# Sixteen stores moved from ScalarE's queue to GpSimd's, and four small moves of work in an attention and experts kernel

## The chip, the cores and the metric

The kernel runs on one core of a Trainium2 chip. The metric is the device time of one execution in microseconds (us), the median of several runs. The engines are TensorE (PE in the profile; PEld is its weight load), VectorE (DVE), ScalarE (ACT), GpSimd (POOL) and SyncE (SP), which issues DMAs. PEq, ACTq and SPq are the engines' sequencers.

## What is computed

The reference chains three blocks (float32; batch B = 2, 768 rows of each, 8 heads of 64, so rows of 512):

```python
# 1. attention: a window of n_local keys behind each row, and n_global keys for all
scores = scale * q @ k.T + bias; scores = where(keep, scores, -1e9)
a = exp(scores - max); a /= sum(a) + 1e-9;  x = a @ v
# 2. one expert of 8 for each row; a row whose local gate is >= 0.5
#    keeps the expert of the row before it
e = argmax(x @ w_gate) if s == 0 or local_gate < 0.5 else prev_e
p = softmax(x @ w_gate);  out[s] = p[e] * (relu(x[s] @ w1[e]) @ w2[e])
# 3. theta, mixing over the 768 rows, output
theta = x @ w_theta; y = w_tok_r @ (x * cos(theta)) + w_tok_i @ (x * sin(theta))
u = x + y; return u + relu(u @ w_ch)
```

## The kernel before

**Attention, 0 to about 99 us.** 24 steps s, each with two units u = 2s and 2s + 1. PE multiplies queries by keys (`s`, L554); DVE adds the bias and takes the maximum in one operation (`sm` with its read-out `st`, L576); ACT exponentiates (`pr`, L586); PE transposes (`pt`, L609); ACT or DVE copies the result (`ps`, L616 and L618); PE multiplies by the values (`x`, L633). Work of a finished block of 128 rows is put at places of later steps by `at(...)`: in an odd step DVE scales the block (`xt`, L659) and later makes the gate logits (`lh`, L231). Each engine takes its instructions in the order in which the code issues them. Two pieces of PSUM are shared in turn by PE's transposes and the small products of the gate, so the second group of `pt` in an odd step can only begin when DVE has read what `lh` reads.

**Jobs.** The weights of block 3 arrive as 64-bit numbers and are turned to float32 bit by bit in "jobs", sequences of one ACT operation (`jm`, L401) and DVE operations (`jw`, L402 to L408; `wtok` L411 and L414). `job_tick()` issues one piece. In attention it is called at the end of the steps in `JATT` (L71).

**Warm products.** Before the first query product PE runs `NWARM` products of a zero tile (`warm`, L858) whose result nobody reads.

**Experts, about 118 to 298 us.** Rows are sorted by expert, gathered from `xd` into tiles (`xg`, L1026, an indirect DMA on POOL), transposed, and run through 8 experts r of 8 parts f each, so u = 8r + f counts 64 parts. The weights `raw` come from SP's queue; ACT and DVE split each into two halves (`w1s` L1346 and L1347, `w2s` L1444 and L1445) for PE (`h` L1463 and L1480, `o` L1536). From r = 4 two parts are run together. `probs()` (L1049 to L1056, seven DVE operations and one of ACT) works out each row's probability once, after part `PU`, and SP stores the table to DRAM (`pd`, L1693). POOL gathers it for each group of rows (`ps`, L1388; for expert 0 from part `GP`). `y_rows` scales an expert's result by it on ACT (`yo`, L1586, two buffers) and stores it to `yd` (L1588). The first 128 rows ("leader's rows") are worked out ahead of the experts in `y0`; `gather_p0` fetches their probabilities after part `HU`, and `y_head` scales and stores them at `HU + 4` (L1591, L1592). At the end POOL gathers rows from `yd` (`rows`, L1408) for `first` (L1428).

**Theta, mix and output, 298 to 476 us**, close to all of it on PE.

Of the kernel before, what the change touches and what calls it, by code (L numbers as in the profile page):

```python
# [50 lines left out]

BLOCKS = [b * NT + t for t in range(NT) for b in range(B)]
TWO_PI = 6.283185307179586
NWARM = 10

WARM = {0: 1, 1: 2, 2: 1, 3: 1, 4: 1}

# [13 lines left out]
JATT = (4, 5, 6, 8, 9, 10, 12, 13, 14, 16, 17, 18, 20, 21, 22)  # L71
# [7 lines left out]
FT = 4  # L79
JF, JL = 4, 56  # L80
LOADS = ((0, 2), (1, 1), (2, 1), (1, 2), (2, 2))
PU = 1
GX = 0
XF = 3
GP = 4
HU = 36
XL = 0
S1A, S1B = 0, 0
C1 = 6.28125
# [11 lines left out]
def kernel(  # L101
# [13 lines left out]
    V, A, G, PE, SP = nc.vector, nc.scalar, nc.gpsimd, nc.tensor, nc.sync  # L115
# [6 lines left out]
    def ct(shape, dt, name):  # L122
        return const.tile(shape, dt, name=name, tag=name)
# [3 lines left out]
    yd = dram.tile([NSLOT * 128, DM], F32, name="yd", tag="yd")  # L127
# [265 lines left out]
    def job(k):  # L393

        t = jraw.pop(k)
        lo, hi = t[:, :, 0], t[:, :, 1]
        w = jtmp.tile([128, 512], I32, tag="jw", name="jw", bufs=1)
        m = jtmp.tile([128, 512], F32, tag="jm", name="jm", bufs=1)
        wf = w.bitcast(F32)
        wh, wl = jobs[k][1]()  # L400
        A.activation(m, hi.bitcast(F32), AF.Abs)  # L401
        V.tensor_scalar(w, hi, 3, 0x3FFFFFFF, op0=ALU.logical_shift_left, op1=ALU.bitwise_and)  # L402
        yield
        V.scalar_tensor_tensor(w, lo, 29, w, op0=ALU.logical_shift_right, op1=ALU.bitwise_or)  # L404
        yield
        V.scalar_tensor_tensor(w, hi, -1073741824, w, op0=ALU.bitwise_and, op1=ALU.bitwise_or)
        yield
        V.scalar_tensor_tensor(wf, m, MIN64, wf, op0=ALU.is_ge, op1=ALU.mult)  # L408
        yield
        wf = wf.rearrange("p (i c) -> p i c", c=wh.shape[-1]) if len(wh.shape) == 3 else wf  # L410
        A.activation(wh, wf, AF.Copy)  # L411
        job_load()
        yield
        jstate["sub"].tensor_tensor(wl, wf, f32(wh), op=ALU.subtract)  # L414

    def job_tick(n=1):
        for _ in range(n):
            if jstate["gen"] is None:
                if jstate["k"] not in jraw:
                    return  # L420
                jstate["gen"] = job(jstate["k"])
                jstate["k"] += 1
            if next(jstate["gen"], 0) == 0:
                jstate["gen"] = None
# [10 lines left out]
    y0 = ct([128, DM], F32, "y0")  # L435
# [6 lines left out]
    with ExitStack() as actx:  # L442
# [11 lines left out]
        def load_qk(i):  # L454
            n = BLOCKS[i]
            b, t = divmod(n, NT)
            q = qs[n] = ab.tile([128, 4, 128], F32, tag="q", name="q", bufs=3)
            src = pack[b, t, :, 0:1152].rearrange("p (j c) -> p j c", j=4)
            o = 0 if t else 32

            for j in (slice(0, 2), slice(2, 4)) if n == 0 else (slice(0, 4),):
                SP.dma_start(q[:, j], src[:, j, 0:128])
                SP.dma_start(kall[:, b, j, t * 160 + o : t * 160 + 160], src[:, j, 128 + o : 288])

        def load_v(i):
            n = BLOCKS[i]
            vv = ab.tile([128, 2, 512], F32, tag="vv", name="vv", bufs=4)
            src = pack[n // NT, n % NT]
            if n % NT:
                SP.dma_start(vv, src[:, 1152:2176].rearrange("p (i c) -> p i c", i=2))  # L470
            else:
                SP.dma_start(vv[:, 1], src[:, 1664:2176])
            vals[n] = vv
# [44 lines left out]
        def biases(t, j):  # L518
            bias, c = (bias1, slice(128, 384)) if t else (bias0, slice(0, 128))
            for h in (2 * j, 2 * j + 1):  # L520
                (G if t else V).tensor_scalar(bias[:, h], drop[:, c], -8.0 * 2.0 ** -(h + 1), None, op0=ALU.mult)
# [22 lines left out]
        def qk(s):  # L544
            n = units[2 * s][0]
            b, t = divmod(n, NT)
            W = 256 if t else 128
            for i in range(2):

                sp = [pS.tile([128, 256], F32, tag=f"s{hh}", name=f"s{hh}") for hh in range(2)]  # L550
                j = units[2 * s + i][1]
                for hh in range(2):
                    half = slice(64 * hh, 64 * hh + 64)
                    PE.matmul(  # L554
                        sp[hh][:, 0:W],
                        lhsT=qs[n][half, j],
                        rhs=kall[half, b, j, t * 160 + 160 - W : t * 160 + 160],
                        start=True,
                        stop=True,
                    )  # L560
                ust[2 * s + i] = {"s": [x[:, 0:W] for x in sp]}
# [291 lines left out]
        def warm(k):  # L853

            if k:
                w = pM.tile([128, 512], F32, tag="m", name="warm")
            for _ in range(k):
                PE.matmul(w, lhsT=wm[:, 0:128], rhs=wm, start=True, stop=True)  # L858
# [53 lines left out]
        def run(names):  # L912
            for k in names.split():
                ops[k]()
# [5 lines left out]

        warm(NWARM)
        biases(0, 0)
# [5 lines left out]
        for s in range(NS):  # L928
            if s % 2 == 0 and s // 2 + 2 < NB and s:
                load_qk(s // 2 + 2)  # L930
                load_v(s // 2 + 2)
            u = 2 * s
            qk(s)
            warm(WARM.get(s, 0))
            run(later.pop((s, 0), ""))
            run(f"sa{u} sb{u}")
            run(later.pop((s, 1), ""))
            if s:
                run(f"tr{u - 2} tr{u - 1} cp{u - 2}")
            run(f"sa{u + 1} sb{u + 1}")  # L940
            if s:
                run(f"cp{u - 1}")
            run(later.pop((s, 2), ""))
            if s == 0:
                biases(0, 2)
                biases(0, 3)
            if s >= 2:
                run(f"pv{u - 4} pv{u - 3}")
                if s % 2:
                    i, t = s // 2 - 1, (s // 2 - 1) // B  # L950
                    at(s + 1, 0, f"ev{i}")
                    at(s + 1, 2, f"ri{i}")
                    at(s + 1, 3, f"yt{i} lg{i}")
                    at(s + 2, 0, f"lc{i} lt{i} ys{i}")
                    at(s + 2, 1, f"ld{i}")
                    if i % B == B - 1:
                        at(s + 2, 2, f"ch{t}")
                        at(s + 3, 0, f"ro{t}")
                        at(s + 3, 1, f"sc{t}")
                        at(s + 4, 0, f"oh{t}")  # L960
                        at(s + 4, 1, f"ho{t}")
                        at(s + 5, 0, f"po{t}")
                        at(s + 5, 1, f"pl{t}")
                        at(s + 5, 2, f"mk{t}")
                        at(s + 6, 3, f"sl{t}")
                        at(s + 7, 1, f"tk{t}")
                        if B * (t + 1) == AHEAD:
                            at(s + 5, 2, "le " + " ".join(f"lw{f}" for f in range(8)))
                            at(s + 7, 1, "lx ls")
            run(later.pop((s, 3), ""))  # L970
            if s in (1, 2):
                job_load()
            if s in JATT:
                job_tick()
            if s in FILLS:
                fill()
# [387 lines left out]
    with ExitStack() as mctx:  # L1364
# [209 lines left out]
        def groups_out(n, M, W):  # L1574

            return yd[n : n + M, :].rearrange("m (g c) -> g m c", c=W)

        def y_rows(r, lo, hi):
            for i in range(lo, hi):
                c = width(r, i)  # L1580
                M = min(128, RCAP[r] - i * 128) if c == 128 else c
                P, W = (M, DM) if c == 128 else (128, 4 * c)
                ps = pslot.pop(RBASE[r] + i)[:P]
                yo = mb.tile([128, DM], F32, tag="yo", name="yo", bufs=2)
                yp = yps[r][i]
                A.activation(yo[:P, :W], yp[:P, :W], AF.Copy, scale=ps)  # L1586
                n = (RBASE[r] + i) * 128
                A.dma_start(groups_out(n, M, W), yo[:P, :W])  # L1588

        def y_head():  # L1590
            A.activation(y0, y0, AF.Copy, scale=pslot.pop(0))  # L1591
            A.dma_start(yd[0:128, :], y0)  # L1592

        def y_last():
            yo = first["yo"] = pre.tile([128, DM], F32, tag="w1s0", name="yo", bufs=3)
# [23 lines left out]
        for u in range(64):  # L1619
# [68 lines left out]
            if GX <= u < GX + RTILES[0]:  # L1688
                gather_x(RBASE[0] + u - GX + 3)
            if u == PU:  # L1690
                probs()
                for b in range(B):
                    SP.dma_start(pd.rearrange("(t b p) o -> b p (t o)", b=B, p=128)[b], ptok[:, b * NT : (b + 1) * NT])  # L1693
            if f == 0:
                slots_of_groups(r)
            i = f - (1 if r else GP)
            if 0 <= i < RTILES[r]:
                gather_p(r, i)
            if u == HU:
                gather_p0()  # L1700
            if u == HU + 4:
                y_head()
# [384 lines left out]
```

## Time and profile before

| | us |
|---|---|
| median of 3 runs (lowest, highest) | 480.87 (480.5, 482.27) |
| profiled execution, whole | 482.78 |
| its span, from first to last instruction | 481.0 |
| attention / rest of its tail / experts / block 3 | 99 / 19 / 180 / 178, then 5 us of stores |

The span is what the profiler's rows cover; 1.8 us lie around it. A row of a timeline has the start, the busy time, the engine, the line, the operation, the tile written and those read, the form, how often it ran in a row, and in brackets how long the engine was idle before it and what released it.

### The profile page before, as it was taken

The page shows a single profiled execution, that of the slowest core. Times are in us where ns is not written, and L with a number is a line of the kernel's source. Part 1 is how long each engine was busy: PE and PEld are TensorE (multiplying, and loading weights), DVE is VectorE, ACT ScalarE, POOL GpSimd, SP SyncE. Part 2 cuts the span into 40 slices and gives each one's busy share as a digit, 9 for nine tenths or more (in the row PEclk, how much of TensorE's full clock was granted, in tenths as well). Part 3 has the DMA queues.
Part 4 walks back from the last instruction along what each step waited for, and adds up shares of the span by engine and source line. Part 5 has one row for each costly group of instructions (what it writes and reads, how often), then busy time and mean ns, then how long its engine had stood idle before and what let it go on. Part 6 is the DMA issues. An engine that isn't in the chain of part 4 may idle for free.

```text
span 481.0 us, 9458 instructions
## 1 busy us (share of the span) xinstructions
PE 467.0 (97%) x3311; PEld 382.3 (79%) x3311; DVE 348.5 (72%) x913; ACT 256.5 (53%) x615; POOL 125.5 (26%) x173
## 2 busy tenths in 40 slices
PE   8999998999999999999999999999999999999995
PEld 4676776778878798888876778788888888888885
DVE  5878878867667788877685876566999899761521
ACT  5978786732445757665555464554655455520300
POOL 8502213224105303020312011203444233340400
PEclk9999999999999999999999999999999999999999
DMA  8978677524939978887998994610012200000022
GB/s 232 369 218 266 180 243 245 196 89 122 348 56 278 312 267 262 291 259 251 292 296 272 314 302 155 188 38 22 23 67 67 65 23 22 1 33 35 33 79 90
DMA packets 62370, 82.96 MB, mean 172 GB/s; under 512 B 6528, under 2 KB 40960, under 8 KB 62320
## 3 DMA queue, kind: packets, MB, share of 16 engines
q1 hardware_dynamic: 54068, 62.66, 40.7%
q10 hardware_dynamic: 5500, 12.85, 7.9%
q0 software_dynamic: 2752, 6.83, 4.9%
q8 instruction: 27, 0.44, 0.4%
q14 instruction: 23, 0.19, 0.1%
HBM read 70.94 MB, written 11.38 MB: 171 GB/s over the span
## 4 chain that ended last, share of the span: by engine, by line
PE 76%; DVE 8%; DMA 7%; ACT 4%; issue 2%; ACTq 1%; SPq 0%; DVEq 0%; POOLq 0%
PE a L1846 21%; PE o L1536 9%; PE h L1480 7%; PE b L1883 7%; PE th L1770 6%; PE h L1463 4%; DMA raw<-in_w_dram 4%; PE x L633 3%; PE s L554 3%; PE pt L609 3%; DMA yd<-yo 3%; DVE sm L576 2%; ACT pr L586 2%; PE y L775 2%; PE h L764 2%
## 5 line engine op out<-in xcount | busy, mean ns | idle before, releaser
L1846 PE MATMUL a<-wtokr,z 128*128 128x512 f32 x480 | 85.9, 337 | 0.0
L1846 PEld LDWEIGHTS a<-wtokr,z 128*128 128x128 f32 x480 | 73.8, 188 | 9.3
L1536 PE MATMUL o<-w2s,hh 128*128 128x512 f32 x192 | 63.6, 409 | 0.8 <-DVE w2s L1445 0.4
L586 ACT ACTIVATE pr<-sm,st 128x256 f32<-128x256 f32 (+1 forms) x96 | 46.0, 481 | 16.7 <-DVE st L576 15.5
L1480 PE MATMUL h<-xT,w1s 128*128 128x288 f32 (+3 forms) x384 | 52.6, 285 | 2.0 <-DVE w1s L1347 1.1
L1480 PEld LDWEIGHTS h<-xT,w1s 128*128 128x128 f32 x384 | 48.8, 189 | 5.8 <-DVE w1s L1347 2.0
L1445 DVE TENSOR_TENSOR w2s<-raw,w2s 128x512 fp32r<-128x512 f32 x56 | 38.5, 687 | 18.9 <-ACT w2s L1444 11.4
L576 DVE CUSTOM_DVE_ANT_0 sm<-s,bias 128x256 f32<-128x256 f32 (+1 forms) x96 | 33.9, 394 | 11.7 <-PE s L554 10.2
L1026 POOL DMA_INDIRECT xg<-xd,xidx x17 | 17.2, 1013 | 95.3 <-PE tr L1318 88.6
L1463 PEld LDWEIGHTS h<-xT,raw 128*128 128x128 f32 x256 | 37.0, 190 | 4.4 <-issue 3.9
L1463 PE MATMUL h<-xT,raw 128*128 128x192 f32 (+3 forms) x256 | 40.5, 311 | 0.0
L1536 PEld LDWEIGHTS o<-w2s,hh 128*128 128x128 f32 x192 | 32.3, 184 | 8.3 <-DVE w2s L1445 2.7
L1536 PE MATMUL o<-w2s,hl 128*128 128x512 f32 x96 | 38.0, 396 | 0.8 <-DVE hl L1511 0.8
L1444 ACT ACTIVATE w2s<-raw 128x512 fp32r<-128x512 f32 x56 | 34.9, 625 | 6.0 <-PE o L1536 3.6
L1347 DVE TENSOR_TENSOR w1s<-raw,w1s 128x512 fp32r<-128x512 f32 x32 | 22.0, 690 | 9.7 <-ACT w1s L1346 9.4
L1891 DVE SCALAR_TENSOR_TENSOR ob<-b,xTf 128x512 f32<-128x512 f32 (+1 forms) x16 | 8.8, 556 | 27.2 <-PE b L1883 27.1
L609 PE MATMUL pt<-ident,pr 128*128 128x128 f32 x176 | 26.1, 281 | 1.8 <-DVE lh L231 0.7
L1802 POOL TENSOR_TENSOR si<-si,yg 128x512 f32<-128x512 f32 x10 | 13.5, 1346 | 51.6 <-ACT si L1795 48.7
L411 ACT ACTIVATE wtokr<-jw 128x512 fp32r<-128x512 f32 x15 | 9.5, 631 | 31.4 <-DVE jw L408 29.5
L554 PE MATMUL s<-kall,q 64*128 64x256 f32 (+1 forms) x192 | 26.0, 388 | 0.1
L404 DVE SCALAR_TENSOR_TENSOR jw<-jraw,jw 128x512 int32<-128x512 int32 x26 | 24.7, 952 | 0.4
L633 PE MATMUL x<-ps,vv 128*64 128x128 f32 x352 | 24.5, 279 | 0.0
(286 smaller groups left out, 952.3 us busy)
## 6 DMA issues: line engine op xcount, KB each, us to landing
raw<-in_w_dram SPq DMA_DIRECT2D x60, 512.0 KB
vv<-in_pack_dram SPq DMA_DIRECT2D x10, 512.0 KB
jraw<-in_w_tokT_dram ACTq DMA_DIRECT2D x10, 512.0 KB
w<-in_w_dram SPq DMA_DIRECT2D x16, 256.0 KB
kall<-in_pack_dram SPq DMA_DIRECT2D x10, 320.0 KB
xd<-xt SPq DMA_DIRECT2D x12, 256.0 KB
q<-in_pack_dram SPq DMA_DIRECT2D x11, 256.0 KB
jraw<-in_w_tokT_dram ACTq DMA_DIRECT2D x10, 256.0 KB
```

The costliest lines, as they stand in the source:

```text
L554: PE.matmul(sp[hh][:, 0:W], lhsT=qs[n][half, j], rhs=kall[half, b, j, t * 160 + 160 - W : t * 160 + 160], start=True, stop=True,)
L576: V.tensor_tensor_reduce(out=sm[:, hh, 0:W], in0=ust[u]["s"][hh], in1=bias[:, 2 * j + hh], scale=-0.125, scalar=BIG, op0=ALU.add, op1=ALU.min,
L586: A.activation(pr[:, hh, 0:W], sm[:, hh, 0:W], AF.Exp, bias=st[:, hh : hh + 1], scale=-1.0, accum_out=sums[n][:, 2 * j + hh : 2 * j + hh + 1],
L609: PE.transpose(pt[:, hh, c], pr[:, hh, c * 128 : (c + 1) * 128], ident)
L633: PE.matmul(xp[64 * hh : 64 * hh + 64, j], lhsT=vv[:, i, h * 64 : (h + 1) * 64], rhs=ps[:, hh, c], start=(c == 0), stop=(c == nch - 1),)
L1444: A.activation(h2, bb[:, o], AF.Copy)
L1445: V.tensor_tensor(l2, bb[:, o], f32(h2), op=ALU.subtract)
L1463: PE.matmul(hp[:, :N], lhsT=pieces[u // 2][1][:, j, o * 128 : (o + 1) * 128], rhs=x[:, j, :N], start=(j == 0), stop=(j == 3),)
L1480: PE.matmul(hp[:, :N], lhsT=wa[:, j], rhs=xa[:, j, :N], start=(k == 0), stop=(k == 11))
L1536: PE.matmul(out[:M], lhsT=ha[:, lo : lo + M], rhs=wa, start=(f == 0 and q == 0), stop=(f == 7 and q == 2),)
L1846: PE.matmul(acc[b][d][o], lhsT=za[:, d * 128 : (d + 1) * 128], rhs=wa[:, lo:hi], start=(t == 0 and n == 0 and (o == 0 or d % 2 == 0)), sto ...
L1883: PE.matmul(op[:, : hi - lo], lhsT=wa[:, d, e * 128 : (e + 1) * 128], rhs=ua[d][:, lo:hi], start=(n == 0), stop=(n == 11),)
```

## The change

Five edits. `NWARM` goes from 10 to 7. `probs()` and the store of its table come after part 3 rather than part 1, and POOL's gathers of expert 0's probabilities start one part later. `gather_p0` comes after part 32 and `y_head` after part 36 rather than 36 and 40. All 16 stores of results to `yd` in `y_rows` and `y_head` are issued by POOL (`G`) rather than ACT (`A`). And the `job_tick()` of an even attention step is issued in the odd step after it, behind that step's first `sm` operations.

```diff
-NWARM = 10
+NWARM = 7
-PU = 1
+PU = 3
-GP = 4
-HU = 36
+GP = 5
+HU = 32
             run(f"sa{u} sb{u}")
+            if s % 2 and s - 1 in JATT:
+                job_tick()
             run(later.pop((s, 1), ""))
...
-            if s in JATT:
+            if s % 2 and s in JATT:
                 job_tick()
...
                 n = (RBASE[r] + i) * 128
-                A.dma_start(groups_out(n, M, W), yo[:P, :W])
+                G.dma_start(groups_out(n, M, W), yo[:P, :W])

         def y_head():
             A.activation(y0, y0, AF.Copy, scale=pslot.pop(0))
-            A.dma_start(yd[0:128, :], y0)
+            G.dma_start(yd[0:128, :], y0)
```

On DVE, in the odd step s = 13 (`jw` is the job, `xt` the scaled block, ISA `sm,st` the bias and maximum, `lh` the gate logits), before:

```order
L600 RECIPROCAL sums<-sums 128x8
L402 TENSOR_SCALAR jw<-jraw 128x512
L659 TENSOR_TENSOR xt<-y,sums 128x512
L576 ISA sm,st<-s_1004,bias_153 128x256
L576 ISA st 128x1
L576 ISA sm,st<-s_1005,bias_153 128x256
L576 ISA st 128x1
L290 TENSOR_TENSOR ohb<-m,rev 128x16
L231 TENSOR_TENSOR lh<-m,sums 128x72
```

and of the change, at the same place:

```order
L600 RECIPROCAL sums<-sums 128x8
L659 TENSOR_TENSOR xt<-y,sums 128x512
L576 ISA sm,st<-s_997,bias_153 128x256
L576 ISA st 128x1
L576 ISA sm,st<-s_998,bias_153 128x256
L576 ISA st 128x1
L402 TENSOR_SCALAR jw<-jraw 128x512
L290 TENSOR_TENSOR ohb<-m,rev 128x16
L231 TENSOR_TENSOR lh<-m,sums 128x72
```

The job's operation has moved from ahead of `xt` and `sm` to between `sm` and `lh`. The same holds in the ten odd steps 5 to 23; in three of them ACT's `jm` moves too, behind the step's first two `pr`.

On POOL, from the gather of expert 1's last tile (`xg`, 112 rows) to those of expert 2 (80 rows), before:

```order
L1026 DMA xg<-xd,xidx 112x512
L1388 DMA ps<-pd,xidx 128x1
L1026 DMA xg<-xd,xidx 128x512
L1388 DMA ps<-pd,xidx 128x1
L1388 DMA ps<-pd,sidx 128x1
L1388 DMA ps<-pd,xidx 128x1 x2
L1026 DMA xg<-xd,xidx 80x512
```

and of the change:

```order
L1028 DMA xg<-xd,xidx 112x512
L1028 DMA xg<-xd,xidx 128x512
L1390 DMA ps<-pd,xidx 128x1 x2
L1390 DMA ps<-pd,sidx 128x1
L1590 DMA yd<-yo 128x512 x2
L1390 DMA ps<-pd,xidx 128x1
L1590 DMA yd<-yo 4x32x128
L1390 DMA ps<-pd,xidx 128x1
L1028 DMA xg<-xd,xidx 80x512
```

Both gathers of rows now stand ahead of the first gather of probabilities, and the stores between the later ones. (Lines from about 937 on are two higher in the change.)

On ACT, around part 40 (`y_107` is the leader's tile `y0`), before:

```order
L1586 ACTIVATE yo<-o,ps 128x512
L1588 DMA yd<-yo 128x512
L411 ACTIVATE wtokr_2116<-jw 128x512
L387 DMA jraw<-in_w_tokT_dram 128x512 x2
L1586 ACTIVATE yo<-o,ps 128x256
L1588 DMA yd<-yo 2x64x256
L1591 ACTIVATE y_107<-y_107,ps 128x512
L1592 DMA yd<-y_107 128x512
L1321 ACTIVATE xT_3898<-tr 128x4x128
```

and of the change:

```order
L1588 ACTIVATE yo<-o,ps 128x512
L411 ACTIVATE wtokr_2113<-jw 128x512
L387 DMA jraw<-in_w_tokT_dram 128x512 x2
L1588 ACTIVATE yo<-o,ps 128x256
L1323 ACTIVATE xT_3895<-tr 128x4x128
```

Three stores and the leader's activation are gone from this stretch; that activation now stands ten rows earlier, behind a `jm` of part 36.

## Rows read from the trace of the kernel before

**Rows 1.** Page part 1: busy time of each engine.

```profile
PE 467.0 (97%) x3311; PEld 382.3 (79%) x3311; DVE 348.5 (72%) x913; ACT 256.5 (53%) x615; POOL 125.5 (26%) x173
```

**Rows 2.** Busy times and counts of each engine, 298 to 476 us.

```profile
298.00:476.00 178.00, 177.44 (x1052) 153.84 (x1052) 121.25 (x193) 72.43 (x138) 51.33 (x39) 1.00 0.17 53
```

**Rows 3.** Timeline of PE and of DVE, the first 7 us.

```profile
1.28 4.45 PE L858 MATMUL warm<-wm 128*128 128x512 bf16 x10 [1.28 <-DVE wm L476]
5.66 0.95 PE L554 MATMUL s<-kall,q 64*128 64x128 f32 x8
...
6.42 0.29 DVE L576 CUSTOM_DVE_ANT_0 sm<-s,bias 128x128 f32<-128x128 f32 x1 [0.69 <-PE s L554]
```

**Rows 4.** Timeline of DVE in attention, step s = 13.

```profile
47.72 0.38 DVE L402 TENSOR_SCALAR jw<-jraw 128x512 int32<-128x512 int32 x1
...
49.03 0.42 DVE L576 CUSTOM_DVE_ANT_0 sm<-s,bias 128x256 f32<-128x256 f32 x1 [0.33 <-PE s L554]
...
49.94 0.23 DVE L231 TENSOR_TENSOR lh<-m,sums 128x72 f32<-128x72 f32 x1
```

**Rows 5.** Timeline of PE weight loads in step s = 7.

```profile
26.04 0.42 PEld L609 LDWEIGHTS pt<-ident,pr 128*128 128x128 f32 x4 [0.22 <-DVE lh L231]
```

**Rows 6.** DVE by line, 20 to 97 us: the most frequent job operation.

```profile
L406 DVE SCALAR_TENSOR_TENSOR jw<-jraw,jw 128x512 int32<-128x512 int32 x3 | 2.2, 742 | 0.0
```

**Rows 7.** Waits from 20 to 97 us: waiter, releaser, total, times, longest.

```profile
DVE sm L576 <- PE s L554: 8.9, 12, 1.4
...
PEld pt L609 <- DVE lh L231: 1.9, 5, 0.4
```

**Rows 8.** Timeline of DVE and PE in parts 1 to 3.

```profile
131.35 0.24 DVE L1049 TENSOR_TENSOR posall<-Lall,mxall 128x96 f32<-128x96 f32 x1
...
133.24 0.69 DVE L1347 TENSOR_TENSOR w1s<-raw,w1s 128x512 fp32r<-128x512 f32 x1
...
138.91 0.69 DVE L1300 TENSOR_TENSOR xT<-tr,xT 128x512 fp32r<-128x512 f32 x1 [2.23 <-ACT xT L1326]
...
133.98 1.19 PE L1480 MATMUL h<-xT,w1s 128*128 128x288 f32 x7 [0.73 <-DVE w1s L1347]
```

**Rows 9.** Timeline of SP, POOL and ACT: the probabilities' way to their use.

```profile
133.35 0.96 SPq L1693 DMA_DIRECT2D pd<-ptok  x2
...
145.47 1.30 POOL L1388 DMA_INDIRECT ps<-pd,xidx  x1 [6.02 <-DMA pd<-ptok]
...
154.86 0.68 ACT L1586 ACTIVATE yo<-o,ps 128x512 f32<-128x512 f32 x1
```

**Rows 10.** Timeline of ACT and PE, part u = 12 and after.

```profile
161.88 1.11 ACTq L1588 DMA_DIRECT2D yd<-yo  x1
...
165.00 1.56 PE L1480 MATMUL h<-xT,w1s 128*128 128x256 f32 x11 [0.41 <-DVE w1s L1347]
```

**Rows 11.** Timeline of ACT, DVE and PE around part u = 40.

```profile
245.73 0.63 ACT L411 ACTIVATE wtokr<-jw 128x512 fp32r<-128x512 f32 x1 [2.87 <-DVE jw L408]
...
254.13 0.72 ACT L1591 ACTIVATE y<-y,ps 128x512 f32<-128x512 f32 x1 [1.64 <-issue]
...
257.16 0.69 DVE L1445 TENSOR_TENSOR w2s<-raw,w2s 128x512 fp32r<-128x512 f32 x1 [5.90 <-ACT w2s L1444]
...
243.46 2.65 PE L1463 MATMUL h<-xT,raw 128*128 128x176 f32 x16
...
248.45 2.65 PE L1463 MATMUL h<-xT,raw 128*128 128x176 f32 x16
...
254.42 2.65 PE L1463 MATMUL h<-xT,raw 128*128 128x176 f32 x16
...
261.62 1.63 PE L1463 MATMUL h<-xT,raw 128*128 128x160 f32 x10
```

**Rows 12.** Timeline of POOL and PE at the end of the experts.

```profile
294.49 0.95 POOL L1408 DMA_INDIRECT rows<-yd,yidx  x1 [16.18 <-DMA yd<-yo]
...
297.89 1.13 PE L1428 MATMUL first<-ident,rows 128*128 128x128 f32 x8 [0.27 <-DMA rows<-yd,yidx]
```

## The prediction

> **What bounds the kernel now.** I read the page's busy times first: PE is busy 467.0 of 481.0 us, so at most 14 us can be won by any reordering, and a change of order can only add to or take from those 14 [rows 1]. The table of stretches comes next. From 298 to 476 us PE is busy 177.44 of 178.00 us [rows 2]: whatever shift PE has at 298 reaches the end one for one, and nothing later can absorb it. So the question is what each edit does to PE's start-to-start times before 298. For that I went through the timelines of PE, and from each gap to the engine that ended it.
>
> The profiled execution took 482.78 us (span 481.0 and 1.8 around it), 1.9 above the median of 480.87. The sum below is a difference, made on the profiled execution and carried to the median unchanged. A difference under 0.5% (2.4 us) can't be told from none in a measurement of this kernel.
>
> **Warm products.** Ten take 4.45 us, from 1.28, so three fewer free PE 1.34 us sooner. The first query product starts at 5.66, DVE's first `sm` at 6.42 after 0.69 us of idleness [rows 3]. The gain can't exceed that idleness, since DVE is busy with the bias until 5.74; the lower bound is nothing, if the second query product's keys are what is late next. I take 0.3, about the middle: **-0.3** (0 to -0.7).
>
> **Job pieces in attention.** This is the largest term. In step 13 of before, DVE runs `jw` at 47.72 and `xt`, and is then idle 0.33 us until PE has the scores: the job is paid from idleness. `lh` follows at 49.94 [rows 4]. Moved behind `sm`, the job delays `lh`, and PE's second transpose group needs `lh`: in step 7 it already waits 0.22 us for it [rows 5], in all five such waits of 1.9 us in sum, so that there is no slack there. DVE's waits for scores in attention are 8.9 us over twelve places [rows 7]: they get longer by what the job no longer fills, and give nothing back. A job's operation has 0.38 us busy for the L402 form [rows 4] and 0.74 on average for the L406 form [rows 6]; consecutive DVE operations overlap by some 0.1, so I count 0.3 and 0.6. There are ten such steps (5 to 23). Going through them with PE's and DVE's rows side by side: where `sm` waited for PE's scores anyway (steps 7, 9, 17), the whole 0.6 is lost, and in step 5, where ACT's `jm` also comes to stand ahead of a copy, 0.5; in step 13 0.3, being the short form; in steps 11, 15, 21 and 23, where the job had made `sm` late, 0.3 to 0.4, because that lateness is won back; in step 19, where it had made it late by more than its own length, nothing. That is 3 x 0.6 + 0.5 + 0.3 + 4 x 0.35 + 0 = 4.0. Some of it will vanish where PE waits a little less for ACT and DVE in the step after: I take **+3.5** (2 to 4.3).
>
> **Probabilities after part 3.** In part 1 the chain of seven DVE operations stands from 131.35 to 133.24 ahead of `w1s`, and PE idles 0.73 us until 133.98; from start to start of the products the gap is 1.03, of which some 0.1 is the product itself. After part 3 DVE is idle 2.23 us before 138.91, which covers the 1.89 of the chain [rows 8]. **-0.95** (-0.7 to -1.0). If that cover were gone, the same 0.95 would be paid there.
>
> **Their way to the use.** Before, the table is stored at 133.35; POOL's first gather waits 6.02 us for it and starts at 145.47, 12.1 us after the store. ACT first needs the gathered values at 154.86 [rows 9]. In the change the chain ends about 138.9 - 0.95 = 137.9; by the same 12.1 us the store lands at 150.0. A gather then has to start (1.3 us) and to land. Before, ACT had 9.4 us from that start to the use; the whole way after would be 159.4, against a use that is now due at 153.9. But that 9.4 held slack that I can't read from a row; at the shortest the gather's own 1.3 us is all (151.3, in time), at the longest all of it counts (5.5 late). ACT is idle at several places in these parts, so a late `yo` becomes lost PE time only in part. I take 1.0 (0 to +3).
>
> **Stores on POOL.** On ACT each store holds up what follows. In part 12 the issue alone takes 1.11 us at 161.88, and PE idles until 165.00, from start to start 0.7 [rows 10]; over the four parts 10 to 13 PE's intervals are some 2.2 us above those of the parts after. Moved to POOL, that queue waits for `yo` instead. Behind it stand gathers for parts four or more later, and POOL is busy 26% of the span [rows 1], so nothing waits for it. The gain here is 0.7 to 2.2, and I take 1.5. With the term above: **-0.5** (-2.2 to +2.3). From 165 to 250 us PE has no idleness of size, and the same edit is worth nothing.
>
> The Trainium skill ("DMA: Bandwidth & Descriptors", Issuing engines are not separate DMA queues) says that the choice of the issuing engine saves only the sequencer's issue time, since all queues share the same DMA engines; that agrees with a gain only where ACT's issue is on the path, as in rows 10. The page's Specifications give about 1 us to the first byte from GpSimd and 0.6 from ScalarE, so by it a store would land 0.4 us later, an estimate.
>
> **The leader's rows and part 40.** Between 254 and 258 us ACT does a store, `y` after 1.64 us of idleness, another store, then the copies for PE; DVE is idle 5.90 us before `w2s` at 257.16. From start to start of PE's first products of two parts it is 7.20 us (254.42 to 261.62), against 5.00 for a quiet pair (243.46 to 248.45) [rows 11]. `y` moves to part 36, where ACT is idle 2.87 us before 245.73 [rows 11] and PE doesn't wait: the 0.72 us of `y` are hidden there. The two stores are gone from ACT. I count most of the 2.2 as won: **-2.0** (-1 to -2.2). A like place at 271 to 277 us, with one store and no `y`, has an excess of 0.4: **-0.4**.
>
> **The end of the experts.** PE waits 0.27 us for the gathered rows at 297.89; the gather starts at 294.49, after 16.18 us of waiting for the last store [rows 12]. A store on its own queue may land sooner, or later: **-0.2** (-0.3 to +1).
>
> Sum: -0.3 + 3.5 - 0.95 - 0.5 - 2.0 - 0.4 - 0.2 = **-0.85**, so 482.78 becomes 481.9, and the median 480.87 becomes **480.0**.
>
> **Rivals.**
>
> *The job pieces cost little.* If DVE catches up before PE's second group comes, because PE is itself late there or because the pieces run in other gaps than I think, that term is 1 or less, and the sum is -3.4 or below: **477.3**. For it: DVE is busy 72% [rows 1], and has 8.9 us of waits nearby [rows 7]. Against it: those waits stand before `sm`, not between `sm` and `lh`.
>
> *The probabilities come late (the slower side).* The store of `pd` takes its 12.1 us again, the gather most of its 9.4 [rows 9]; ACT stands at its first `yo`, and behind it, in order, the splits of the weights for PE. Then that place costs +3 rather than -0.5, and with the job pieces at 4.0 the sum is +3.2: **484.0**. It decides from the point where the first gather starts later than about 150 us. For it: 12 us is what the row has. Against it: the transfers of weights may be thinner at that time.
>
> *The clock starts later.* The warm products take 0.445 us for 512 columns, 1.2 columns per ns, which is the lower of the two clocks (1.2 and 2.4 GHz) [rows 3]. Fewer of them could let the query products run longer at it; eight took 0.95 us, so one more group at that speed costs up to 0.5 and two 1.0: the sum is about 0, **481.0**, no change. The table of stretches has the granted clock as 1.00, but in a stretch that does not show the first microseconds [rows 2]. The Trainium skill ("TensorE: Matmul & The Clock Gate", Part 1) has the throttled clock as the default that activity releases, which speaks for this rival; no run here shows it with fewer products.
>
> *The gap at part 40 stays*, since the copies there wait for something else than ACT's order: +1.7 on the sum, **481.7**, no change.
>
> **How the numbers follow.** Forecast 0.35, job pieces cheap 0.33, probabilities late 0.18, clock 0.07, part 40 stays 0.07. The forecast's own range, by its terms' bounds taken together half way, is 478 to 482; the rivals' times widen it to **476.5 to 484.5**. Faster by over 0.5% (below 478.5): most of the second case and a tenth of the first, 0.34. Slower (above 483.3): the third and a little of the others, 0.20. The rest, 0.46, is within.
>
> **What would show it.** In the changed profile: DVE's wait for scores in attention grows from 8.9 us, PE's wait for `lh` from 1.9 to about 5, and the tail begins some 3 us later; if both stay, the largest term falls. PE runs through part 1 without the 0.73 us; POOL's gather starts at 149 to 151, and the first `yo` stands before or after it. ACT's rows at part 40 follow without the stores, and the pair takes 5 us. A first query product before 5 us with `sm` below 6.2 shows the warm term. The prediction is wrong above all if the job pieces or the probabilities' lateness are off by more than 2.5 us.

## The result: 1.07% slower

The median went from 481.66 us (12 runs) to **486.69 us** (12 runs, 485.17 to 489.63). The ratio is 1.0107, with a 95% interval of 1.0079 to 1.0135. The forecast was 480.0 with a range to 484.5: outside, on the slower side. The profiled execution took 488.08 us, its span 486.3, so 1.8 us lie around it as before.

Of the page, part 1 and the clock's line of part 2 (40 slices of 12.2 us):

```profile
PE 467.1 (96%) x3308; PEld 385.4 (79%) x3308; DVE 349.0 (72%) x913; ACT 257.2 (53%) x615; POOL 138.7 (29%) x189
...
PEclk9999999999999799999999999999999999999999
```

PE's busy time is what it was (467.1 against 467.0, [rows 1]); the span is longer, so PE idles more. One slice, the fourteenth (158 to 170 us), has a granted clock of 0.7.

Where the time went is read by comparing PE's starts: the start of PE's first product at a place in the change's timeline, less that in the kernel before. Each row of this table is worked out from two such rows of the timelines; the middle column is what the place added.

| place | change less before, us | added | what lies between |
|---|---|---|---|
| step 4 | +0.59 | +0.59 | warm products |
| step 23 | +3.83 | +3.24 | job pieces |
| part 2 | +4.36 | +0.53 | tail, first weights |
| part 6 | +3.38 | -0.98 | probabilities out of part 1 |
| part 11 | +3.38 | 0 | |
| part 13 | +10.16 | +6.78 | the first use of the probabilities |
| part 16 | +8.63 | -1.53 | ACT behind the late table, stores |
| part 46 | +8.67 | 0 | |
| part 48 | +6.46 | -2.21 | leader's rows, stores |
| part 56 | +5.16 | -1.30 | stores off ACT |
| last instruction | +5.32 | +0.16 | |

Most of these are close to what the terms of the sum said, and one is far off. The last column says what lies at a place; whether it is the cause is settled only by the experiments.

**The late probabilities.** Timelines of SP, POOL, ACT and PE of the change:

```profile
141.98 0.96 SPq L1695 DMA_DIRECT2D pd<-ptok  x2
...
156.54 0.94 POOL L1390 DMA_INDIRECT ps<-pd,xidx  x1 [10.28 <-DMA pd<-ptok]
...
163.39 0.69 ACT L1588 ACTIVATE yo<-o,ps 128x512 f32<-128x512 f32 x1 [6.43 <-DMA ps<-pd,xidx]
...
164.65 3.44 PE L1482 MATMUL h<-xT,w1s 128*128 128x256 f32 x12 [3.94 <-ACT w1s L1348]
```

The table is stored at 141.98. POOL's first gather starts at 156.54, 14.6 us later ([rows 9]: 12.1). ACT stands at its first `yo` for 6.43 us, until the gathered values have landed, and starts it at 163.39, 6.85 us after the gather's start. Behind `yo` in ACT's order is `w1s` for part 12, so PE idles 3.94 us. And then the clock falls. Busy times by stretch of the change (PE, PEld, DVE, ACT, POOL, granted clock, DMA share, GB/s):

```profile
157.00:159.00 2.00, 2.00 (x16) 1.85 (x15) 0.42 (x1) 0.00 (x0) 1.43 (x2) 1.00 0.99 352
159.00:161.00 2.00, 1.71 (x9) 1.10 (x7) 0.00 (x0) 0.00 (x0) 0.95 (x1) 1.00 1.06 375
161.00:163.00 2.00, 0.00 (x0) 0.00 (x0) 0.00 (x0) 0.00 (x0) 0.00 (x0) 1.00 1.08 345
163.00:165.00 2.00, 0.35 (x1) 0.29 (x1) 0.37 (x1) 1.61 (x3) 0.61 (x1) 0.66 0.77 237
165.00:167.00 2.00, 1.86 (x8) 1.62 (x8) 1.66 (x4) 2.00 (x6) 0.21 (x1) 0.50 0.88 343
167.00:169.00 2.00, 2.00 (x9) 1.81 (x8) 1.95 (x5) 1.39 (x4) 1.48 (x2) 0.50 0.44 166
169.00:171.00 2.00, 2.00 (x9) 1.51 (x9) 0.31 (x1) 0.45 (x2) 0.88 (x2) 0.63 0.84 257
```

PE is idle from 160.7 to 164.65; from about 163.6 to 170.5 the granted clock is 0.50, the lower of the two levels (1.2 against 2.4 GHz), and PE is busy from 164.65 on. So 4.10 us are added before part 12's start, by idleness, and 2.68 between its start and part 13's, where the products run at the slower clock.

**Job pieces.** Step 13 on DVE, then two waits from 20 to 101 us, then PE's weight loads in step 7:

```profile
51.52 0.42 DVE L576 CUSTOM_DVE_ANT_0 sm<-s,bias 128x256 f32<-128x256 f32 x1 [0.40 <-PE s L554]
...
52.21 0.08 DVE L576 DVE_READ_ACCUMULATOR2_ANT st<- 128x1 f32 x1
...
52.63 0.22 DVE L231 TENSOR_TENSOR lh<-m,sums 128x72 f32<-128x72 f32 x1
```

```profile
DVE sm L576 <- PE s L554: 10.0, 15, 1.4
...
PEld pt L609 <- DVE lh L231: 6.1, 9, 1.0
```

```profile
27.81 0.42 PEld L609 LDWEIGHTS pt<-ident,pr 128*128 128x128 f32 x4 [0.82 <-DVE lh L231]
```

The job now stands between `sm` and `lh`. PE's wait for `lh` went from 1.9 us over five places to 6.1 over nine, and DVE's wait for scores from 8.9 to 10.0 [rows 7]; in step 7 it is 0.82 us against 0.22 [rows 5]. (PE's two rows of a wait, of loads and of products, overlap and aren't added.)

**Parts 5 and 6.** PE and DVE:

```profile
137.32 1.76 PE L1482 MATMUL h<-xT,w1s 128*128 128x288 f32 x12
...
141.37 1.83 PE L1482 MATMUL h<-xT,w1s 128*128 128x288 f32 x12
...
139.97 0.25 DVE L1051 TENSOR_TENSOR posall<-Lall,mxall 128x96 f32<-128x96 f32 x1
...
142.29 0.69 DVE L1302 TENSOR_TENSOR xT<-tr,xT 128x512 fp32r<-128x512 f32 x1 [0.34 <-ACT xT L1328]
```

PE runs through part 5 without the 0.73 us of [rows 8]. The chain of seven operations begins at 139.97, in the stretch in which DVE had been idle 2.23 us [rows 8], and the copy behind it follows at 142.29, still after 0.34 us of idleness.

**Part 40 and the end.** ACT and PE around the place of [rows 11], then POOL and PE at the end of the experts:

```profile
249.99 0.71 ACT L1593 ACTIVATE y<-y,ps 128x512 f32<-128x512 f32 x1
...
257.12 2.65 PE L1465 MATMUL h<-xT,raw 128*128 128x176 f32 x16
...
263.09 2.65 PE L1465 MATMUL h<-xT,raw 128*128 128x176 f32 x16
...
268.08 2.44 PE L1465 MATMUL h<-xT,raw 128*128 128x160 f32 x16
```

```profile
300.31 1.08 POOL L1410 DMA_INDIRECT rows<-yd,yidx  x1 [5.04 <-DMA yd<-yo]
...
303.89 1.13 PE L1430 MATMUL first<-ident,rows 128*128 128x128 f32 x8 [0.92 <-DMA rows<-yd,yidx]
```

`y` is in part 36's slack, and the pair takes 4.99 us (263.09 to 268.08) against 7.20. At the end PE waits 0.92 us for the gathered rows against 0.27 [rows 12].

### The profile page after: what moved, and what is told of

The parts are those of the page before. It is cut to its first block, busy times and chain, and to the rows that moved or that the text cites. A ratio compares the mean times of both kernels' runs of the same rounds, so it can differ in the third digit from the quotient of the medians.

```text
span 486.3 us, 9451 instructions
## 1 busy us (share of the span) xinstructions
PE 467.1 (96%) x3308; PEld 385.4 (79%) x3308; DVE 349.0 (72%) x913; ACT 257.2 (53%) x615; POOL 138.7 (29%) x189
## 4 chain that ended last, share of the span: by engine, by line
PE 75%; DMA 8%; DVE 8%; issue 3%; ACT 3%; POOL 3%; ACTq 0%; SPq 0%; DVEq 0%; POOLq 0%
PE a L1848 21%; PE o L1538 9%; PE h L1482 7%; PE b L1885 7%; PE th L1772 6%; PE h L1465 4%; PE x L633 4%; PE s L554 3%; PE pt L609 3%; DMA pd<-ptok 3%; DVE sm L576 2%; PE h L764 2%; PE y L775 2%; DMA yd<-yo 1%; DMA ps<-pd,xidx 1%
## 5 line engine op out<-in xcount | busy, mean ns | idle before, releaser
L1482 PEld LDWEIGHTS h<-xT,w1s 128*128 128x128 f32 x384 | 50.0, 193 | 7.8 <-ACT w1s L1348 4.4
L1590 POOL DMA_DIRECT2D yd<-yo x15 | 9.6, 643 | 81.9 <-ACT yo L1588 81.9
L1349 DVE TENSOR_TENSOR w1s<-raw,w1s 128x512 fp32r<-128x512 f32 x32 | 21.9, 687 | 13.4 <-ACT w1s L1348 13.0
L1804 POOL TENSOR_TENSOR si<-si,yg 128x512 f32<-128x512 f32 x10 | 13.4, 1345 | 51.4 <-ACT si L1797 48.5
L609 PEld LDWEIGHTS pt<-ident,pr 128*128 128x128 f32 x176 | 19.7, 143 | 9.7 <-DVE lh L231 6.9
```

Source lines behind the costliest of these rows:

```text
L609: PE.transpose(pt[:, hh, c], pr[:, hh, c * 128 : (c + 1) * 128], ident)
L1482: PE.matmul(hp[:, :N], lhsT=wa[:, j], rhs=xa[:, j, :N], start=(k == 0), stop=(k == 11))
```

## The experiments

Each was timed beside the kernel before on the same chip (481.25 to 481.71 us), and its ratio is to that; where two experiments are compared, the difference of the ratios stands beside that of the medians. "Place" numbers below are PE's starts less those of the kernel before in its profiled execution, as in the table above.

**e1: the probabilities back.** Of the change:

```diff
-PU = 3
+PU = 1
-GP = 5
+GP = 4
```

> The change with the probabilities back after part 1 and their gathers from part 4. Account from the traces: PE's parts 12 and 13 lost 6.8 us to the late table of probabilities, and the earlier place won 1.0; undone together the run is 5.8 us below the change, about 480.9 us, and level with the kernel before; POOL's first gather starts near 147 us and ACT has no wait of several us for it. Rival: the stores on POOL's queue are what makes the gathers late, wherever the table is stored; then 484 to 487 us.

Measured: 486.65 us, ratio 1.0122 (1.008 to 1.0164). The miss is not in the span: it was 479.7, and parts 12 and 13 lost nothing (+2.70 at parts 11 and 12, +2.33 at part 13). But 5.7 us lay around the span, not 1.8. The wait is gone as the account says; the time came back after the last instruction, which e8 and e9 take up.

**e2: the job pieces alone.** Of the kernel before, the two hunks of `job_tick` of the change.

> The kernel before with the job pieces moved behind the first sm, nothing else. Account from the traces: the odd steps 5 to 23 of attention grow by 3.2 us in sum, so about 484.9 us, 0.7% above before. Rival: the steps grew because the start of attention (fewer warm products) upset the order of the engines; then this run is within 0.5 us of before.

Measured: 485.06 us, ratio 1.0072 (1.0049 to 1.0094). Between step 4 and step 23 PE's starts fall back by 3.27 us, as in the change by 3.24, and the wait for `lh` is the same:

```profile
PEld pt L609 <- DVE lh L231: 6.2, 9, 1.0
```

The job pieces cost 3.3 us in the profile and 3.5 in the median. The rival falls.

**e3: stores and leader's rows alone.** Of the kernel before:

```diff
-HU = 36
+HU = 32
-                A.dma_start(groups_out(n, M, W), yo[:P, :W])
+                G.dma_start(groups_out(n, M, W), yo[:P, :W])
...
-            A.dma_start(yd[0:128, :], y0)
+            G.dma_start(yd[0:128, :], y0)
```

> The kernel before with the 16 stores on POOL and the leader's rows four parts sooner, nothing else. Account from the traces: parts 13 to 16 win 1.5 us and parts 47 to 56 win 3.5, so about 476.6 us, 1.0% below before. Rival: the stores on POOL's queue delay its gathers, so that part 12 waits as in the change; then 480 us or more.

Measured: 482.45 us, ratio 1.002 (0.9998 to 1.0042). The span is 477.4, 3.5 us shorter; part 12 doesn't wait (-0.21), PE wins 1.04 us between the starts of parts 12 and 16, 2.21 between 46 and 48 and 0.44 from there to 56. So the stores don't make the gathers late. The third `yo` has to wait for a store to land, longer than in the kernel before (of which the first row is):

```profile
161.48 0.37 ACT L1586 ACTIVATE yo<-o,ps 128x128 f32<-128x128 f32 x1 [0.47 <-DMA yd<-yo]
```

```profile
161.51 0.37 ACT L1586 ACTIVATE yo<-o,ps 128x128 f32<-128x128 f32 x1 [2.05 <-DMA yd<-yo]
```

Around the span there are 5.2 us here too, which takes the gain away.

**e4: seven warm products alone** (`NWARM = 7` in the kernel before).

> The kernel before with seven warm products, nothing else. Account from the traces: TensorE stays at the lower clock until 9.5 us rather than 6, and the fifth step's products start 0.6 us later, so about 482.3 us. By the prediction's own term 481.4. Rival: the late start spreads through attention, 485 us.

Measured: 481.04 us, ratio 0.9993 (0.9968 to 1.0018). In this execution step 4 began 0.75 us sooner, not later. The profiled executions with seven products fall in two groups: in four (e1, e4, e6, e9) step 4 is 0.71 to 0.76 sooner than in the kernel before, in two (the change and e12) 0.54 to 0.59 later. With ten products it lies between 0.74 sooner and 0.08 later. The median shows no effect.

**e5: the probabilities alone** (`PU = 3`, `GP = 5` in the kernel before).

> The kernel before with the probabilities after part 3 and their gathers from part 5, nothing else. Account from the traces: PE wins 1.0 us at part 6, and ACT then waits some 6 us for the gathered probabilities at part 8's result, so that PE loses about 4 us of idleness and 2.7 of lower clock: about 487.4 us. Rival: the table is late only together with the other edits (the shifted queue of SP, the stores on POOL); then 480.6 to 483 us.

Measured: 484.99 us, ratio 1.0083 (1.005 to 1.0117), in single runs 483.11 to 488.87. SP, POOL and ACT:

```profile
137.72 1.34 SPq L1693 DMA_DIRECT2D pd<-ptok  x2
...
151.16 1.04 POOL L1388 DMA_INDIRECT ps<-pd,xidx  x1 [9.15 <-DMA pd<-ptok]
...
156.92 0.69 ACT L1586 ACTIVATE yo<-o,ps 128x512 f32<-128x512 f32 x1 [4.22 <-DMA ps<-pd,xidx]
```

Store to gather 13.4 us, ACT's wait 4.22, and parts 12 and 13 lost 4.34 us; PE idled 2.33 us, and the granted clock behind it was 0.59 from 159 to 161 us and 0.56 from there to 163. The rival falls: the late table needs none of the other edits. It is less late here than in the change, so the size is 2.4 us below what was expected. From part 13 to part 16 PE wins back 1.59 us, with all stores still on ACT.

**e6: the table stored from ACT's queue.** Of the change:

```diff
-                    SP.dma_start(pd.rearrange("(t b p) o -> b p (t o)", b=B, p=128)[b], ptok[:, b * NT : (b + 1) * NT])
+                    A.dma_start(pd.rearrange("(t b p) o -> b p (t o)", b=B, p=128)[b], ptok[:, b * NT : (b + 1) * NT])
```

> The change, with the store of the table of probabilities issued on ACT's queue rather than SP's. If it was late because it stood behind the transfers of weights, in SP's order and in its queue, it now lands in some 3 us and ACT's wait is gone: about 480 us. If its 1536 pieces of 4 bytes take their 12 us in any queue, it lands 2 us sooner than in the change only, and a wait of some 4 us of ACT's 6.4 stays: 483 to 485 us.

Measured: 484.15 us, ratio 1.0063 (1.0037 to 1.0088). Rows of ACT's queue, POOL and ACT:

```profile
140.75 1.00 ACTq L1695 DMA_DIRECT2D pd<-ptok  x2
...
152.37 0.94 POOL L1390 DMA_INDIRECT ps<-pd,xidx  x1 [7.23 <-DMA pd<-ptok]
...
158.22 0.69 ACT L1588 ACTIVATE yo<-o,ps 128x512 f32<-128x512 f32 x1 [1.10 <-DMA ps<-pd,xidx]
```

The way from store to gather is 11.6 us on a queue that carries nothing else then: the second theory. It is three microseconds shorter than on SP's queue in the change, and that is enough: ACT waits 1.10 us, and part 12 begins with 0.07 us lost, the clock at 1.00 throughout. So the lateness has an edge, and the change lay some 5 us past it. What is left against the kernel before is the job pieces' 3.3 us; the stores win nothing here, PE even loses 0.9 us between the starts of parts 12 and 14, where the third `yo` waits 2.84 us until a store on POOL's queue has landed.

**e7: all that won.** The kernel before with e3's edits, `PU = 3`, `GP = 5` and e6's store.

> The kernel before with the stores on POOL, the leader's rows sooner, the probabilities after part 3, and their table stored from ACT's queue; ten warm products and the job pieces as before. By the sum of the parts -1.5 - 3.5 - 1.0: a span of about 475.5 us if the table is in time on ACT's queue, 478 to 480 if it needs its 12 us there too. The time around the span is 1.8 us by the account that it depends on where the code ends, 5.2 if the stores on POOL bring it.

Measured: 480.83 us, ratio 0.9987 (0.9967 to 1.0008). Span 479.4, 1.8 us around it. The way from store to gather is 11.9 us, ACT still waits 1.12 us, parts 12 and 13 lose 0.7 (the third `yo` waits 2.30 us for a store on POOL's queue), and of the 2.4 us won up to part 62, 0.8 go at the end of the experts.

**e8: e3 with one instruction more on GpSimd.**

```diff
         G.memset(toks, 0.0)
+        G.memset(toks, 0.0)
```

> The run with stores on POOL and leader's rows sooner, plus one small memset on GpSimd at the start, so that its program has one instruction more. That run had a span of 477.4 us and 5.2 us around it, with instruction fetches of all engines 3 us after the last instruction. If the place where the code ends decides over that fetch, one instruction can take it away: a span of 477.4 and 479.2 us in all. If the stores on POOL bring it: 482.5 us as before.

Measured: 478.94 us, ratio **0.9973** (0.9947 to 0.9998): 3.5 us below e3 for one more instruction (2.3 by the ratios). The span was 478.7 in this execution and 1.9 us lay around it. In e7, too, the stores are on POOL and 1.8 us lie around the span, so the stores don't bring the 5.2.

**e9: e1 with the same extra instruction.**

> The change with the probabilities back after part 1, plus one small memset on GpSimd, so that the 3.4 us of instruction fetches after the end (seen with the probabilities back, 5.7 us around the span) go away. By the account: 486.65 - 3.5 = 483.1 us, so that the late table costs the change some 3.5 us net in an average execution, 5.8 in the profiled one. Rival: the time around the span has nothing to do with the program's length; then 486.6 us.

Measured: 482.53 us, ratio 1.0042 (1.0019 to 1.0066), 1.8 us around the span. So the probabilities' move cost the change 486.69 - 482.53 = 4.2 us net of the 1.0 it won (3.1 by the ratios). From the parts one would expect e9 nearer 481; two waits for transfers, ACT's for the first weights and PE's for the gathered rows, have grown:

```profile
131.33 0.63 ACT L1349 ACTIVATE w1s<-raw 128x512 fp32r<-128x512 f32 x1 [3.65 <-DMA raw<-in_w_dram]
...
298.05 1.13 PE L1431 MATMUL first<-ident,rows 128*128 128x128 f32 x8 [1.04 <-DMA rows<-yd,yidx]
```

In the kernel before, the first was 2.11 us, and the second is 0.27 [rows 12].

**e10: one part later instead of two.** e8 with `PU = 2`.

> The fastest run so far (kernel before, stores on POOL, leader's rows sooner, one memset more: 478.9 us), with the probabilities one part later than before rather than two, gathers from part 4. The table then leaves about 2 us later than before and lands near 147.5 by its 12 us; the first gather starts before 148 and lands before 154, in time. If DVE has as much room after part 2 as after part 3, PE wins 1.0 us: 478.0 us. If the chain of seven operations holds up DVE there as in part 1: 478.9 us.

Measured: 479.09 us, ratio 0.997 (0.9951 to 0.999). Part 6 wins 1.0 and part 12 loses nothing (-0.02 on both), so the place is right; but PE's wait for the gathered rows at the end rose to 1.84 us, and the time is e8's.

**e11: the leader's rows alone** (`HU = 32` in the kernel before).

> The kernel before with the leader's rows four parts sooner, nothing else. The stores and the leader's rows together won 2.2 us between parts 46 and 48. By the prediction's reading (y on ACT, its 1.64 us of idleness and its own store are most of the gap) 1.5 to 2 us are won here alone: 480 us. Rival: the gap there is the stores' wait on ACT; then this run gives 0.5 us or less, 481.2 us.

Measured: 480.86 us, ratio 0.999 (0.9971 to 1.0009). Parts 46 to 48 win 1.66 of the 2.21 us. That looks like the prediction's reading, but it doesn't show it: e5, e4 and e2, which leave the leader's rows where they were and the stores on ACT, win 1.64, 1.50 and 0.90 us at the same place. Their rows of `y` (e4, e5, e2), which waited 1.64 us in the kernel before [rows 11]:

```profile
251.78 0.72 ACT L1591 ACTIVATE y<-y,ps 128x512 f32<-128x512 f32 x1 [0.61 <-ACT yo L1586]
```

```profile
254.98 0.72 ACT L1591 ACTIVATE y<-y,ps 128x512 f32<-128x512 f32 x1 [0.61 <-ACT yo L1586]
```

```profile
255.47 0.72 ACT L1593 ACTIVATE y<-y,ps 128x512 f32<-128x512 f32 x1 [0.81 <-DMA raw<-in_w_dram]
```

Most of the gap is thus that one execution's own, and what the leader's rows alone win isn't shown. The gain of this run is given back at the end of the experts, where PE came sooner and the store on ACT's queue didn't land sooner:

```profile
297.69 1.13 PE L1428 MATMUL first<-ident,rows 128*128 128x128 f32 x8 [1.59 <-DMA rows<-yd,yidx]
```

**e12: the wait filled.** The change with products that keep PE busy ahead of part 12; they write a tile that the next product overwrites:

```diff
                 prods = ((h1, xh), (l1, xh), (h1, xl))
+                if u == 12:
+                    for _ in range(16):
+                        PE.matmul(hp, lhsT=xh[:, 0, :128], rhs=xh[:, 1:3, :N], start=True, stop=True)
```

> The change with 16 products of 512 columns, whose result is overwritten, ahead of part 12's first product, where PE idled 3.9 us and the granted clock then fell to 0.50 for 6.8 us. They take some 3.7 us at the high clock. If the idleness is what lowers the clock, it now stays at 1.00, parts 12 to 14 run at full speed, and about 2.5 us come back although PE has 3.7 us more to do: part 13 starts 7.5 us later than before rather than 10.2, and about 484.5 us. Rival: the clock falls there for another reason (then 486.7 us or more), or the products hold PE up where the table is in time (488 us).

Measured: 484.11 us (ratio 1.0071, 1.0043 to 1.0099), 2.6 us below the change (1.7 by the ratios, whose intervals overlap) with 3.81 us more for PE to do. Busy times by stretch, columns as above:

```profile
159.00:161.00 2.00, 2.00 (x11) 1.65 (x10) 0.00 (x0) 0.00 (x0) 0.00 (x0) 1.00 1.06 356
161.00:163.00 2.00, 2.00 (x11) 1.64 (x10) 0.39 (x1) 1.63 (x3) 0.61 (x1) 1.00 0.96 300
163.00:165.00 2.00, 2.00 (x15) 1.81 (x14) 1.66 (x4) 2.00 (x6) 0.23 (x1) 1.00 0.96 370
165.00:167.00 2.00, 2.00 (x14) 1.70 (x13) 2.00 (x5) 1.71 (x4) 1.47 (x2) 1.00 0.47 171
167.00:169.00 2.00, 2.00 (x18) 1.96 (x17) 1.07 (x3) 1.55 (x4) 1.57 (x2) 1.00 0.93 269
```

The clock stays at 1.00, and part 13 starts 6.51 us later than before, not 10.16 (in this execution the gathered values also came sooner: ACT waited 4.58 us, not 6.43).

## Why the prediction was wrong

The edits and their places were read rightly. One term failed by its size, in a mechanism that a rival had named, and a price behind it was left out; two other terms came near their places in the profile by luck.

- **"Their way to the use": +1.0 (0 to +3). This step failed.** Its place measured +6.78 us in the profiled execution. Less the 3.38 us by which PE was late there anyway, the table's store left at 138.6 (137.9 said), the gather started 14.6 us after it (12.1 said), ACT was due at 153.6 (153.9 said), and the gather's values came 6.85 us after its start. That last step is the largest error: the term's lower end had "the gather's own 1.3 us", by which ACT waited for nothing, and of its range to 3 only 1.0 was taken. In the six runs in which ACT's first `yo` waits for the values (the change, e5, e6, e7, e10, e12) it starts 5.8 to 6.9 us after the gather, so of the 9.4 us before some 2.5 to 3.6 were slack. That a late `yo` is lost for PE only in part was right: ACT waited 6.43 us and PE 3.94. The store's way is 11.6 and 11.9 us on ACT's queue (e6, e7) and 12.1 on SP's after part 2 (e10), so some 12 us belong to it wherever it is issued; why it took 13.1 to 14.6 on SP's queue after part 3 (e12, e5, the change) stays open. The rival on the slower side had the mechanism and its edge (a first gather after 150 us); its price of +3 is near the idleness, and lacked what comes after.
- **No term had the clock behind a wait.** The sum took PE's busy time as fixed: "a change of order can only add to or take from those 14". Of the 6.78, 2.68 are products at the lower clock after 3.94 us of idleness. e12 shows the cause: with the idleness filled the clock didn't fall, and from part 12's start to part 13's it took 3.15 us (164.02 to 167.17) rather than 6.17.
- **Stores on POOL: -1.5.** PE won 1.53 between the starts of parts 13 and 16, so that the term of -0.5 came out as +5.25; but that the stores won it isn't shown, and the nearness is luck. Between these parts e5, e4 and e2, with their stores on ACT, win 1.59, 1.43 and 1.19 us; with stores on POOL e9, e1 and e3 win 1.46, 0.90 and 0.67, and e10 and e6 lose 0.34 and 0.57. Against the stores stands a wait that the prediction didn't count: `yo` has two buffers, and the third waits until the first has been stored, 1.3 to 3.1 us in e1, e3 and e6 to e10 (stores on POOL), 0 to 1.2 in the kernel before, e2, e4 and e11 (on ACT). From that first store's issue to its landing, as the third `yo` shows it, it took 6.2 to 7.5 us on POOL's queue in those seven, 5.8 and 6.6 on ACT's in the kernel before and e11.
- **Job pieces: +3.5 (2 to 4.3).** Measured +3.24 in the change and +3.27 alone. By steps: 0.5 in step 5 (0.5 said), 0.6 in step 7 (0.6), 0.46 and 0.47 in 9 and 17 (0.6), 0.30, 0.27, 0.20 and 0.06 in 11, 15, 21 and 23 (0.35), 0.20 in 13 (0.3), 0.28 in 19 (0). The rival that DVE would catch up falls with e2.
- **Probabilities out of part 1: -0.95.** Measured -0.98, and -1.00 in e5.
- **Leader's rows and part 40: -2.0, and -0.4 behind it.** The places measured -2.21 and, to part 56, -1.30. The first was priced from a gap that the same code doesn't repeat: 0.9 to 1.6 us of it are gone in e2, e4 and e5 without either edit, so the two edits together are worth some 0.6 to 1.3 there, and the nearness to -2.0 is luck. In all nine runs with both edits the place measures 2.21 or 2.22, so the rival that the gap stays has no support; how much the leader's rows have in it stays open. The second is the stores': from part 48 to 56 every run with stores on POOL wins 0.1 to 1.3 us, and none with stores on ACT does.
- **The end of the experts: -0.2.** PE waited 0.92 us for the rows rather than 0.27, and the place as a whole added 0.16.
- **Warm products: -0.3.** +0.59 in the profiled execution, and no effect in the median of e4.

On the rival of the late clock: it is seen in that execution's first rows of PE (the first fence), compared with those of e9, which has the same seven products:

```profile
1.29 3.17 PE L858 MATMUL warm<-wm 128*128 128x512 bf16 x7 [1.29 <-DVE wm L476]
4.73 1.23 PE L554 MATMUL s<-kall,q 64*128 64x128 f32 x8 [0.28 <-DMA kall<-in_pack_dram]
...
6.47 1.43 PE L554 MATMUL s<-kall,q 64*128 64x128 f32 x8
...
8.66 1.06 PE L609 MATMUL pt<-ident,pr 128*128 128x128 f32 x4
```

```profile
4.57 1.00 PE L555 MATMUL s<-kall,q 64*128 64x128 f32 x8
...
6.20 0.94 PE L555 MATMUL s<-kall,q 64*128 64x128 f32 x8 [0.32 <-DVE st L577]
...
7.52 0.63 PE L610 MATMUL pt<-ident,pr 128*128 128x128 f32 x4
```

Eight query products at 6.47 take 1.43 us and four transposes at 8.66 take 1.06 in the change; in e9 they take 0.94 and 0.63. The late clock is thus one of two kinds of start after the same seven products, seen in two of six traces with seven and in none of eight with ten, and e4's median shows no effect; whether fewer products make it more frequent stays open. The Trainium skill ("TensorE: Matmul & The Clock Gate", Part 1) has the slow clock as the state from which activity frees the engine; the rows agree.

With the places as measured, -0.85 becomes +5.3, the span's difference (0.53 of it between step 23 and part 2, for which the sum had no term). The ratios, which don't hang on one execution, give for each edit alone +3.5 us for the job pieces (e2), +4.0 for the probabilities (e5), -0.3 and no effect for the warm products (e4), and -1.3 (-2.6 to -0.1) for the stores and the leader's rows together (e8; -2.8 by the medians), where the prediction's terms make -4.1. They add up to +5.8, against +5.2 for the change, which is within their intervals. So the prediction was wrong on both sides: the late table cost more than was said, and the stores and leader's rows won less.

What stays open: why single executions of the change differ by 4.5 us (their spans 483.4 to 487.7, with mean clocks of 0.996 to 0.990; the longer ones have the lower clock, which fits a table that lands now sooner, now later, but only one of them has a trace).

The fastest kernel of the study is e8 (0.9973), level with e10 (0.997): stores on GpSimd and the leader's rows sooner, without the moves of the probabilities by two parts, of the job pieces and of the warm products.

## What to carry to other kernels

When a producer is moved later, work out the whole way to its first reader, the landing of each transfer included, and compare the end with the time at which the reader is due; a row's issue time says nothing about landing. Price an idle stretch of TensorE with the slower products behind it, which here were another two thirds of the idleness. Before a gap is priced, see whether a second execution has it: the gap at part 40 was mostly one execution's. And work that fills an engine's wait for another engine is free only there: the same job operations behind that wait, ahead of something that TensorE needs, cost 3.2 us over ten steps, in step 7 the full 0.6.

## What the runs showed of the hardware that was not expected

The time around the span can change with the length of a program. Two kernels with 282 GpSimd instructions in their traces (e1, e3) had 5.7 and 5.2 us around the span, with five packets on the queues of instructions 2.8 to 3.6 us after the last instruction; with 283 (the change, e6 to e9, e12), 284 (e10) or 266 (the others) it was 1.8 to 1.9 and no such packet came. One memset more took 3.5 us (e3 to e8) and 4.1 us (e1 to e9) off the medians, 2.3 and 3.9 by the ratios. That these fetches of instructions make up the 3.4 us is read from their times; which boundary the programs' end falls on was not tried.

Also, 1536 pieces of 4 bytes needed 11.0 to 14.6 us from the issue of the store to the end of POOL's wait in all fourteen traces, although in the kernel before the trace's packet records have nearly all of them done 2 us after the issue.
